# Last linear-attention layer: denominators by groups of four tiles, reciprocals spread by DMA

## The chip, the cores and the metric

The kernel runs on one core of a Trainium2 chip. The metric is the time of one execution in device microseconds (us). Five engines run side by side, each with its own instruction order: TensorE (PE in the profile, its weight loads PEld), VectorE (DVE), ScalarE (ACT), GpSimd (POOL) and SyncE (SP), which here issues the DMAs.

## The reference

The input x has 2048 rows of 512 channels. Four layers follow one another, each with its own layer norm and residual: A, B, A, B. A is softmax attention with 32 heads of width 16 and one shared key and value head. B is linear attention, and its second use, the last layer, is what the change is about.

```python
def _B_ref(x, wqkv, wo):
    ...
    phi = lambda t: jnp.where(t > 0, t + 1, jnp.exp(t)) + 1e-6
    pq, pk = phi(q), phi(k)
    kv = jnp.einsum("bhsd,bhse->bhde", pk, v)
    z = jnp.einsum("bhsd->bhd", pk)
    num = jnp.einsum("bhqd,bhde->bhqe", pq, kv)
    den = jnp.einsum("bhqd,bhd->bhq", pq, z)[..., None] + 1e-6
    o = num / den
    return (lambda x, *d: x.transpose(*d))(o, 0, 2, 1, 3).reshape(B, S, D) @ wo
...
x = A_x
x = x + _A_ref(_layernorm(x, axis=-1), A_wq, A_wk, A_wv, A_wo)
x = x + _B_ref(_layernorm(x, axis=-1), B_wqkv, B_wo)
x = x + _A_ref(_layernorm(x, axis=-1), A_wq, A_wk, A_wv, A_wo)
x = x + _B_ref(_layernorm(x, axis=-1), B_wqkv, B_wo)
```

kv and z sum over all 2048 rows, so no row of a layer B can leave before the last row of the layer A ahead of it has come through.

## The kernel before

The rows are 16 tiles of 128. x stays in SBUF in bf16 over all layers. The program numbers the layers 0 to 3; layers 0 and 2 are A, layers 1 and 3 are B.

**A planner writes the order.** The kernel's Python code doesn't write instructions in the order in which they run. It describes each operation with its engines and their durations, the data that it reads and writes, and a priority, and a small event simulation in the class Planner chooses each engine's order: on a free engine the ready operation with the lowest priority number goes first. Then every engine's list is emitted with semaphore waits where one engine needs another's result. On the chip the order of each engine is fixed, and an instruction that waits holds up all behind it on its engine. The planner's durations are constants of the code; a DMA that spreads reciprocals counts as DBI = 0.7 us on SP and DBL = 1.6 us more until its data are there. TABLE is a list of times on the planner's own clock, at each of which some of its constants take new values: BLS (how much work may wait for VectorE before it takes another block of exponentials), AHEAD, CHT, STICK, HTOL and the like.

**Layers 0 and 2** (run_a) are products of queries and keys on TensorE (line 1205), exponentials, and products with the values (line 1259). The exponentials of 128 x 512 blocks are shared: most go through ScalarE (line 1402), others through an integer approximation on VectorE (line 1506), for which GpSimd makes three shifted copies (line 1548).

**Layers 1 and 3** (run_b) run beside the softmax layer ahead of them as far as their tiles are there: tile_ makes the norm, k and v of a tile, q_ its phi(q) in QT, kvt adds kv and z over groups of tiles (line 1811 z, line 1814 kv). When the last tile has come through, the end stage of a layer B begins, in which nothing of a layer A runs beside layer 3:

- kvt's last group masks kv to its heads' blocks (kvT, line 1847). mix multiplies it with the output weights, into four 128 x 512 matrices M, which are copied from PSUM to SBUF (line 1870). In layer 3 all four copies are on VectorE (MCOP), in layer 1 two of them are on ScalarE (MCO1).
- The denominators of layer 3 are made by den3, for tiles in pairs (DG). z is copied (zs, line 1841) and built into the block matrix Zbd (lines 1844 and 1845), whose 128 columns repeat each head's sum 16 times. So the product of Zbd with QT (line 1895) gives every denominator already spread to the 16 channels of its head. ScalarE takes the logarithm (line 1898) and the exponential of its negative (line 1902), 512 columns per tile, and VectorE multiplies QT by it (line 1906).
- The denominators of layer 1 are made by denc, for four tiles together (DENC). z is masked to ZC (line 1833) and ZD (line 1837), in which each head stands once, and one column-tiled product (line 1929) puts the 8 x 4 heads of four tiles into one PSUM bank. One logarithm (line 1933) and one exponential (line 1934) of that bank give the compact reciprocals rec of the four tiles. norm1 then spreads them to 128 partitions. For tiles 0 to 3 and 12 to 15 (PEX) TensorE does it with a matrix E4 (lines 1972 and 1975), and VectorE multiplies from PSUM (line 1980). For tiles 4 to 11 a DMA on SP's queue writes them to a buffer in SBUF (line 1959), and VectorE multiplies from there (line 1962). The buffers are a pool of three (rb_pool), rec has a pool of two (rec_pool).
- main3 multiplies each tile with the four matrices M (line 878), VectorE adds the result to x (line 2011), and SP stores the tile (line 2036).

The two lines that spread the reciprocals of a tile by DMA and use them:

```python
d = op({SP: (DBI, lambda e: e.dma_start(rb, rec[32 * j:32 * j + 8, :].unsqueeze(1).to_broadcast([8, DH, D])))}, ...
o = op({DV: (0.34, lambda e: e.tensor_tensor(out=q, in0=q, in1=rb, op=ALU.mult))}, ...
```

Of the kernel before, what the change touches and what calls it, by code (L numbers as in the profile page):

```python
# [420 lines left out]
class Seg:  # L421
# [128 lines left out]
MCOP = (DV,)*4  # L550
# [6 lines left out]
PEX = (12, 13, 14, 15)  # L557
# [31 lines left out]
BASE = dict(AHEAD=AHEAD, BLS=BLS, BLT=BLT, BLX=BLX, CHT=CHT, DPP=DPP, DXB=DXB, EVP=EVP, FBS=FBS, HMAX=HMAX, HTOL=HTOL, LOW=LOW, OWNP=OWNP, SPX=SPX, STICK=STICK)  # L589


def bass_interleave_layers__grouped_kv_mqa__linear_attn_block__prompt_kernel(
# [41 lines left out]
    zs = sb("zs", [P, 4], FP32)  # L634
# [1043 lines left out]
    rb_pool = Pool_((6, 7, 8))  # L1678
    rec_pool = Pool_((4, 5))
    rd_pool = Pool_(range(6))  # L1680

    def run_b(L):
# [76 lines left out]
        def q_(t):  # L1759
# [10 lines left out]
            if L == 3 and t == T - 1 and QCL:  # L1770
                claim(PAIRS, "pair")
# [9 lines left out]
        def kvt(gi, ts):  # L1781
# [47 lines left out]
            if end:  # L1829
                mk = mask8[:, :, 0:DH]  # L1830
                v4 = lambda x: x.rearrange("p g (h c) -> p g h c", c=DH)
                if L == 1:
                    o = op({DV: (0.13, lambda e, b=bs[1]: e.tensor_tensor(
                        out=ZC[:].rearrange("p (g c) -> p g c", c=40)[:, :, 0:8], in0=bank(b, 4).unsqueeze(2).to_broadcast([P, 4, 8]),
                        in1=mask8[:, :, 0:1].rearrange("p h o -> p (h o)").unsqueeze(1).to_broadcast([P, 4, 8]), op=ALU.mult))},
                           reads=["mask8"], writes=[B_(bs[1]), "ZC"], prio=pr - 0.05)
                    op({DV: (0.1, lambda e: e.tensor_copy(ZD[:].rearrange("p (g c) -> p g c", c=32)[:, :, 0:8], ZC[:].rearrange("p (g c) -> p g c", c=40)[:, :, 0:8]))},
                       reads=["ZC"], writes=["ZD"], prio=1.6)
                    pl.process(denc(0, DENC[0], bs[1]))
                else:  # L1840
                    o = op({DV: (0.08, lambda e, b=bs[1]: e.tensor_copy(zs[:], bank(b, 4)))}, writes=[B_(bs[1]), "zs"], prio=pr - 0.05)
                    pl.give_after(banks, bs[1], [o])
                    for g in range(4):
                        op({AC: (0.19, lambda e, g=g: e.activation(v4(Zbd)[:, g], mk, ACTF.Copy, scale=zs[:, g:g + 1]))} if g in ZAC else
                           {DV: (0.11, lambda e, g=g: e.tensor_scalar(out=v4(Zbd)[:, g], in0=mk, scalar1=zs[:, g:g + 1], scalar2=None, op0=ALU.mult))},
                           reads=["mask8", "zs"], writes=[("Zbd", g)], prio=0.5 if g in ZAC else pr - 0.05, over=under(ZI))
# [9 lines left out]
        ZK = [("Zbd", g) for g in range(4)]  # L1856
        at = {3: lambda i: W[:, i, :], 1: vm_}[L]
        MK = {3: lambda i: ("W", i), 1: lambda i: ("vm", i)}[L]
        ZI, KI = {3: (44, 45), 1: (4, 5)}[L]
        Zbd = at(ZI).rearrange("p (g c) -> p g c", c=P)  # L1860
# [13 lines left out]

        def take_pairs():
            yield ("flag", TPF)
            claim(PAIRS, "pair")

        def den3(ts):
            pr = 1.5 + 0.02 * ts[0] - 0.01  # L1880
            yield ("flag", ("kv", L, len(KVG) - 1))
            for t in ts:
                yield ("flag", ("bq", L, t))
            yield from until(*[QK_(t) for t in ts], *ZK)
            i = yield ("acq", rd_pool, pr)
            n = len(ts)
            rd = wv_(4 * (5 + i), 4).bitcast(FP32)[:, 0:512 * n]
            b = yield ("acq", pairs if n == 2 else banks, pr)
            src = ps[:, b * 512:(b + n) * 512]
            bk = [B_(b + k) for k in range(n)]  # L1890
            for k, t in enumerate(ts):
                def fn(e, k=k, t=t):
                    ins = None
                    for g in range(4):
                        ins = e.matmul(ps[:, (b + k) * 512 + g * P:(b + k) * 512 + (g + 1) * P], lhsT=Zbd[:, g, :], rhs=QT[:, t, g * P:(g + 1) * P], start=True, stop=True)
                    return ins
                op({PE: (0.23, fn)}, reads=[QK_(t)] + ZK, writes=[bk[k]], prio=pr, lat=0.2).cols = 512
            o = op({AC: (0.203 + 0.427 * n, lambda e: e.activation(rd, src, ACTF.Ln, bias=epsc[:]))}, reads=["epsc"], writes=bk + [("rd", i)], prio=pr,
                   after=[("W", 20 + 4 * i + h) for h in range(4)])
            pl.give_after(pairs if n == 2 else banks, b, [o])  # L1900
            rb = wv_(PT0 + 3 * i, n)
            op({AC: (0.148 + 0.427 * n, lambda e: e.activation(rb, rd, ACTF.Exp, scale=-1.0))}, reads=[("rd", i)], writes=[("rb", i)], prio=pr - (EXF if ts[0] < EXN else EXB), after=[("W", PT0 + 3 * i + h) for h in range(n)])
            os_ = []
            for k, t in enumerate(ts):
                qn = W[:, 4 + t, :]
                os_.append(op({(PO if t in PQ else DV): (PQD if t in PQ else 0.34, lambda e, t=t, k=k, qn=qn: e.tensor_tensor(out=qn, in0=rb[:, 512 * k:512 * (k + 1)], in1=QT[:, t, :], op=ALU.mult))},
                              reads=[("rb", i), QK_(t)], writes=[("qn", t)], prio=pr, after=[("W", 4 + t)]))
                pl.flag(("qn", L, t))
            pl.give_after(rd_pool, i, os_)

        def denc(gi, ts, b=None):
# [28 lines left out]
            if gi:  # L1940
                pl.give_after(banks, b, [o])
                yield ("flag", ("rd1", gi))
# [6 lines left out]
        def norm1(t, i, j, rec, b=None):  # L1949
            pr = 1.5 + 0.02 * t - 0.005 if t else DCP  # L1950
            yield from until(("rec", i))
            if DW[t] is not None:
# [3 lines left out]
            if t >= 4 and t not in PEX:  # L1956
                k = yield ("acq", rb_pool, pr)
                rb = vm_(k) if k < 8 else rbx[:]
                d = op({SP: (DBI, lambda e: e.dma_start(rb, rec[32 * j:32 * j + 8, :].unsqueeze(1).to_broadcast([8, DH, D])))},
                       reads=[("rec", i)], writes=[("rb", k)], prio=pr, lat=DBL, dma=True, over=[("va", k)] if k < 8 else [])  # L1960
# [3 lines left out]
                pl.give_after(rb_pool, k, [o])  # L1964
# [19 lines left out]
            if used[t // 4] == 4:  # L1984
                yield ("ops", [m])
                pl.flag(("rd1", t // 4))

        def main3(t):
# [8 lines left out]
            qn = QT[:, t, :] if L == 1 else W[:, 4 + t, :]  # L1997
# [84 lines left out]
```

## Time and profile before

| what | us |
|---|---|
| median of 3 runs | 1339.75 (1339.72 to 1339.89) |
| the profiled execution | 1339.58 |
| its span, first to last instruction | 1338.1 |
| TensorE, ScalarE, VectorE, GpSimd busy in the span | 1291.6, 1308.2, 1233.7, 1097.9 |

The profile is of one execution. A group's row names the line, the engine, the operation, output and inputs with their shapes and the count, then its busy time and the mean ns of one instruction, then the engine's idle time just ahead of it and what ended that. A row of the timeline gives start and length in us, and several like instructions in a row are one row with their count (x4); in brackets stands a wait ahead of it. A row of a stretch gives its length, each engine's busy time with the number of instructions, the granted TensorE clock, the mean busy share of the 16 DMA engines and their GB/s. SPq is SP's DMA queue; the length there is that of the issue, not of the transfer.

### The profile page before, as it was taken

To read this page: it belongs to the slowest core of one execution; us is meant where nothing else is said; L and a number is where in the kernel's file an instruction comes from. 1 tells how busy PE (TensorE), PEld (TensorE's weight loads), DVE (VectorE), ACT (ScalarE), POOL (GpSimd) and SP (SyncE) were. 2 spreads that over 40 slices of the span, in tenths; PEclk is the share of its full clock that TensorE was granted. 3 is DMA by queue.
4 is the path that set the end of the run, shared out by engine and by line. 5 is a ranking of instruction groups with operands and counts; after the bars stand their busy time and mean duration, and the time that the engine had idled before them with its cause. 6 is when DMAs were issued, how large, how long until landed. Compare 5 with 4: busy or idle time off the path is not lost.

```text
span 1338.1 us, 39100 instructions
## 1 busy us (share of the span) xinstructions
PE 1291.6 (97%) x15353; PEld 430.6 (32%) x15411; DVE 1233.7 (92%) x2227; ACT 1308.2 (98%) x1524; POOL 1097.9 (82%) x1107
## 2 busy tenths in 40 slices
PE   9999999999999999999999999999999999999998
PEld 5222323222232223223732223333233323232235
DVE  8999999999999999997889999999999999999987
ACT  8999999999999999999799999999999999999996
POOL 3799897999989998997017999779899898988980
PEclk9999999999999999999999999999999999999999
DMA  4300000000000000000121000000000000000001
GB/s 112 96 6 13 6 13 6 6 13 2 14 5 14 6 6 6 2 2 2 24 38 21 1 10 10 18 6 6 13 6 9 6 14 6 10 2 1 2 2 64
DMA packets 47076, 20.11 MB, mean 15 GB/s; under 512 B 39728, under 2 KB 46384, under 8 KB 46896
## 3 DMA queue, kind: packets, MB, share of 16 engines
q1 hardware_dynamic: 45840, 17.57, 6.0%
q8 instruction: 125, 2.05, 0.6%
q14 instruction: 55, 0.45, 0.1%
q10 hardware_dynamic: 1056, 0.03, 0.0%
HBM read 5.28 MB, written 2.10 MB: 6 GB/s over the span
## 4 chain that ended last, share of the span: by engine, by line
PE 52%; ACT 30%; issue 8%; DVE 7%; POOL 2%; DMA 1%; SPq 0%; ACTq 0%; POOLq 0%
ACT W L1402 28%; PE ps L1259 22%; PE ps L1205 17%; PE ps L878 4%; DVE W L1506 3%; PE ps L1084 3%; POOL W L1548 2%; PE ps L921 2%; PE ps L1306 1%; ACT phE L1688 1%; DMA va<-va 1%; DVE sacc L1566 1%; PE ps L1814 0%; DMA rbx<-va 0%; DVE st L981 0%
## 5 line engine op out<-in xcount | busy, mean ns | idle before, releaser
L1548 POOL INT64_ADD W<-W x1065 | 1089.2, 1038 | 202.5 <-PE ps L1306 64.8
L1402 ACT ACTIVATE W<-ps 128x1024 bf16<-128x1024 f32 (+1 forms) x1317 | 1245.2, 1131 | 2.4 <-PE ps L1205 2.3
L1506 DVE TENSOR_SCALAR W<-ps 128x512 int16<-128x512 f32 x1420 | 921.6, 682 | 64.9 <-PE ps L1205 50.7
L1259 PE MATMUL ps<-W,VV 128*32 128x512 bf16 x8356 | 635.9, 384 | 4.4 <-DVE sacc L1566 2.8
L1205 PE MATMUL ps<-W,KM 32*128 32x512 bf16 x4096 | 517.3, 385 | 23.2 <-ACT W L1402 13.7
L1205 PEld LDWEIGHTS ps<-W,KM 32*128 32x128 bf16 x4096 | 130.3, 91 | 513.0 <-ACT W L1402 428.4
L1259 PEld LDWEIGHTS ps<-W,VV 128*32 128x32 bf16 x8356 | 151.7, 94 | 257.2 <-issue 170.0
L878 PE MATMUL ps<-wqkv,W 128*128 128x512 bf16 (+1 forms) x226 | 66.0, 368 | 7.7 <-issue 4.3
L1306 PE MATMUL ps<-W,V 128*32 128x512 bf16 (+5 forms) x184 | 52.0, 346 | 0.3 <-DVE W L1506 0.2
L1688 ACT ACTIVATE phE<-ps 128x512 bf16<-128x512 f32 (+1 forms) x66 | 43.8, 665 | 4.5 <-PE ps L1084 3.0
L981 DVE BATCH_NORM_STATS2 st<-x_sb 128x6 f32<-128x512 bf16 x60 | 40.5, 679 | 1.2 <-DMA x_sb<-in_A_x_dram 1.2
L1566 DVE STREAM_TRANSPOSE sacc<-ps 128x512 f32<-128x512 f32 x52 | 36.8, 707 | 3.0 <-PE ps L1259 3.0
L921 PE MATMUL ps<-wo,OT 128*32 128x512 bf16 (+1 forms) x544 | 39.4, 372 | 0.0
L1084 PE MATMUL ps<-W,wqkv 128*128 128x128 bf16 x512 | 38.9, 220 | 0.4 <-DVE W L1695 0.3
L1084 PE MATMUL ps<-W,wq 128*128 128x128 bf16 x464 | 35.1, 221 | 0.4 <-DVE W L1506 0.2
L1084 PEld LDWEIGHTS ps<-W,wqkv 128*128 128x128 bf16 x512 | 29.6, 98 | 11.0 <-issue 8.1
L786 DVE TENSOR_SCALAR phE<-phE 128x513 bf16<-128x513 bf16 x49 | 20.7, 423 | 12.8 <-ACT phE L1688 11.7
L1084 PEld LDWEIGHTS ps<-W,wq 128*128 128x128 bf16 x464 | 26.1, 98 | 12.5 <-issue 8.4
L878 PEld LDWEIGHTS ps<-wqkv,W 128*128 128x128 bf16 x272 | 18.1, 97 | 32.1 <-issue 20.1
L786 DVE TENSOR_SCALAR xn<-x_sb,mv,rs 128x513 bf16<-128x513 bf16 x52 | 26.8, 526 | 0.5 <-ACT rs L972 0.5
L1605 DVE TENSOR_TENSOR Osb<-sacc,ps 128x256 bf16<-128x256 f32 x64 | 26.0, 406 | 0.3
L2011 DVE TENSOR_TENSOR x_sb<-x_sb,ps 128x512 bf16<-128x512 bf16 x30 | 20.4, 682 | 2.5 <-PE ps L878 2.1
(140 smaller groups left out, 483.0 us busy)
## 6 DMA issues: line engine op xcount, KB each, us to landing
out_dram<-x_sb SPq DMA_DIRECT2D x16, 128.0 KB, 1.7
x_sb<-in_A_x_dram SPq DMA_DIRECT2D x6, 256.0 KB, 5.8
wqkv<-in_B_wqkv_dram SPq DMA_DIRECT2D x1, 1536.0 KB, 7.4
va<-va SPq DMA_DIRECT2D x6, 128.0 KB
W<-xn SPq DMA_TRANSPOSE x46, 2.5
x_sb<-in_A_x_dram SPq DMA_DIRECT2D x4, 128.0 KB, 2.2
wq<-in_A_wq_dram SPq DMA_DIRECT2D x1, 512.0 KB, 4.4
wo<-in_A_wo_dram SPq DMA_DIRECT2D x4, 128.0 KB, 3.5
```

The costliest lines, as they stand in the source:

```text
L786: return e.add_instruction(mybir.InstTensorScalarPtr(name=nc.get_next_instruction_name(), engine=mybir.EngineType.DVE, op0=op0, op1=op1, i ...
L878: return e.matmul(dst, lhsT=l, rhs=r, start=(k == 0), stop=(k == len(pairs) - 1))
L921: ins = e.matmul(ps[32 * q:32 * q + 32, b * 512 + cs.start:b * 512 + cs.stop], lhsT=l[:, q, :], rhs=r, start=start, stop=stop)
L1084: ins = e.matmul(dst[:, g * P:(g + 1) * P], lhsT=lhs(g, k), rhs=rhs(k), start=(k == 0), stop=(k == FT - 1))
L1205: return e.matmul(bank(b), lhsT=KM[r, sg.par, kt * P:(kt + 1) * P], rhs=QT[r, sg.t, :], start=True, stop=True)
L1259: ins = e.matmul(ps[32 * j:32 * j + 32, ACC * 512:(ACC + 1) * 512], lhsT=VV[:, kt, 0 if w is None else 1 + w, :], rhs=ap, start=(k == 0), ...
L1306: o = op({PE: (n / 2400.0, lambda e: e.matmul(ps[32 * j:32 * j + 32, b * 512:b * 512 + n], lhsT=V0[:], rhs=QT[:, sg.t, 0:n], start=st, sto ...
L1402: ex = op({AC: (EXO + 0.4267 * n, lambda e, n=n, s_=s_, p_=p_: e.activation(ws_(p_), ps[:, s_ * 512:(s_ + n) * 512], ACTF.Exp, scale=EXPSC ...
L1506: o = op({DV: (0.602, lambda e: e.tensor_scalar(out=dst.bitcast(I16), in0=bank(b), scalar1=VB, scalar2=VLO, op0=ALU.add, op1=ALU.max))}, w ...
L1548: o = op({PO: (512 * m * PSR + PSO, lambda e, g_=g_, f_=f_: e.int64_add(ws_(g_).bitcast(I64), ws_(f_).bitcast(I64), step))}, reads=wk_(f_) ...
L1566: o = op({DV: (TRD, lambda e, src=src: e.transpose(src, bank(ACC)))}, writes=[B_(ACC)] + key, prio=0.0, lat=0.15)
L1688: op({AC: (0.07 + n / 1200.0, lambda e: e.activation(phE[:, i, 0:n], bank(b, n), ACTF.Exp))}, reads=[B_(b)], writes=[("phE", i)], prio=pr ...
```

## The change

Layer 3 takes layer 1's way to the denominators: denc and norm1 serve both, and den3, take_pairs, zs and Zbd go, and with them the pairs of PSUM banks that were set aside for den3. ZC and ZD are made in layer 3 too. Tiles 0 to 3 are spread by TensorE, all of tiles 4 to 15 by DMA (PEX is empty for layer 3), with eleven buffers in place of three. VectorE multiplies in place in QT, where den3 wrote to other blocks. The copies of M take turns between VectorE and ScalarE. In TABLE the entries from 1140 on are replaced by two, at 1110 and 1140, and AHEAD, BLT, CHT and OWNP are no longer varied.

```diff
-MCOP = (DV,)*4
+MCOP = (DV, AC, DV, AC)
...
-PEX = (12, 13, 14, 15)
+PEX = {1: (12, 13, 14, 15), 3: ()}
...
-    (1140, dict(BLS=1.6, BLT=2.5, BLX=2.4, DPP=1.0, DXB=0.0, EVP=0.95, FBS=22, HMAX=0.1, HTOL=0.0, LOW=20, STICK=1.0)),
-    (1170, dict(AHEAD=32, BLS=1.6, BLT=2.5, BLX=2.4, DPP=1.0, DXB=-1, EVP=0.95, FBS=22, HMAX=0.1, HTOL=0.0, LOW=20, OWNP=1.0, STICK=1.0)),
-    (1290, dict(AHEAD=32, BLS=1.6, BLT=2.5, BLX=2.4, CHT=11, DPP=1.0, DXB=-1, EVP=0.95, FBS=22, HMAX=0.1, HTOL=0.0, LOW=20, OWNP=1.0, SPX=1.5, STICK=0.5)),
+    (1110, dict(BLS=1.6, BLX=2.4, DPP=1.0, DXB=0.3, EVP=0.95, FBS=22, HMAX=0.1, HTOL=0.02, LOW=20, STICK=1.0)),
+    (1140, dict(BLS=1.9, BLX=2.4, DPP=1.0, DXB=-1, EVP=0.95, FBS=22, HMAX=0.1, HTOL=0.0, LOW=20, STICK=1.0)),
...
-    rb_pool = Pool_((6, 7, 8))
+    rb_pools = {1: Pool_((6, 7, 8)), 3: Pool_((6, 7, 8) + tuple(range(20, 28)))}
     rec_pool = Pool_((4, 5))
-    rd_pool = Pool_(range(6))
...
-            if L == 3 and t == T - 1 and QCL:
-                claim(PAIRS, "pair")
...
-                if L == 1:
-                    o = op({DV: (0.13, lambda e, b=bs[1]: e.tensor_tensor(
...
-                    pl.process(denc(0, DENC[0], bs[1]))
-                else:
-                    o = op({DV: (0.08, lambda e, b=bs[1]: e.tensor_copy(zs[:], bank(b, 4)))}, writes=[B_(bs[1]), "zs"], prio=pr - 0.05)
...
+                o = op({DV: (0.13, lambda e, b=bs[1]: e.tensor_tensor(
...
+                pl.process(denc(0, DENC[0], bs[1]))
...
-        def take_pairs():
...
-        def den3(ts):
...
-            if t >= 4 and t not in PEX:
-                k = yield ("acq", rb_pool, pr)
-                rb = vm_(k) if k < 8 else rbx[:]
+            if t >= 4 and t not in PEX[L]:
+                k = yield ("acq", rb_pools[L], pr)
+                rb = vm_(k) if k < 8 else rbx[:] if k == 8 else W[:, k, :]
...
-            qn = QT[:, t, :] if L == 1 else W[:, 4 + t, :]
-            keys = [("qn", t)] + [("M", g) for g in range(4)] + [QK_(t)] * (L == 1)
+            qn = QT[:, t, :]
+            keys = [("qn", t)] + [("M", g) for g in range(4)] + [QK_(t)]
...
-        if L == 3:
-            pl.process(take_pairs())
-            for ts in DG:
-                pl.process(den3(ts))
-        else:
-            for gi, ts in enumerate(DENC):
-                if gi:
-                    pl.process(denc(gi, ts))
+        for gi, ts in enumerate(DENC):
+            if gi:
+                pl.process(denc(gi, ts))
```

More of the change, by code (lines that the diff above doesn't have):

```diff
@@ L1873, in mix @@
             pl.flag(("M", L, g))
-        def take_pairs():
-            yield ("flag", TPF)
-            claim(PAIRS, "pair")
-        def den3(ts):
[L1880 to L1909, printed above, removed]
         def denc(gi, ts, b=None):
@@ L1951, in norm1 @@
             yield from until(("rec", i))
-            if DW[t] is not None:
+            if L == 1 and DW[t] is not None:
                 yield ("flag", ("xnT", 2, DW[t]))
@@ L1955, in norm1 @@
             q = QT[:, t, :]
[L1956 to L1958 removed]
+            if t >= 4 and t not in PEX[L]:
+                k = yield ("acq", rb_pools[L], pr)
+                rb = vm_(k) if k < 8 else rbx[:] if k == 8 else W[:, k, :]
                 d = op({SP: (DBI, lambda e: e.dma_start(rb, rec[32 * j:32 * j + 8, :].unsqueeze(1).to_broadcast([8, DH, D])))},
[L1960 removed]
+                       reads=[("rec", i)], writes=[("rb", k)], prio=pr, lat=DBL, dma=True, over=[("va", k)] if k < 8 else [], after=[("W", k)] if k > 8 else [])
                 yield ("ops", [d])
```

28 lines of the change are left out of this document (10 added, 18 removed).

## The prediction

> **What bounds the kernel now.** I read the page first, then the stretches, then the chain and the timeline behind the last exponential, and last the place where the kernel already does in layer 1 what the change brings to layer 3.
>
> ```profile
> PE 1291.6 (97%) x15353; PEld 430.6 (32%) x15411; DVE 1233.7 (92%) x2227; ACT 1308.2 (98%) x1524; POOL 1097.9 (82%) x1107
> ...
> L1402 ACT ACTIVATE W<-ps 128x1024 bf16<-128x1024 f32 (+1 forms) x1317 | 1245.2, 1131 | 2.4 <-PE ps L1205 2.3
> L1506 DVE TENSOR_SCALAR W<-ps 128x512 int16<-128x512 f32 x1420 | 921.6, 682 | 64.9 <-PE ps L1205 50.7
> ```
>
> Busy times of the whole span, then two groups with count, busy time and mean ns: ScalarE and TensorE are full over the span, and most of it is the softmax exponentials, shared by ScalarE (L1402) and VectorE (L1506). The last exponential ends at about 1303. The change touches what lies behind it, and the planner's constants in the last 190 us ahead of it. In stretches (columns PE, PEld, DVE, ACT, POOL, clock, DMA share, GB/s):
>
> ```profile
> 1110.00:1303.20 193.20, 187.97 (x2283) 59.11 (x2284) 177.10 (x311) 193.20 (x221) 172.92 (x169) 1.00 0.02 4
> ```
> ```profile
> 1315.00:1320.00 5.00, 4.72 (x49) 3.23 (x51) 4.50 (x10) 4.97 (x6) 0.00 (x0) 1.00 0.00 2
> 1320.00:1325.00 5.00, 4.95 (x46) 3.14 (x46) 4.62 (x12) 5.00 (x6) 0.00 (x0) 1.00 0.36 119
> 1325.00:1330.00 5.00, 4.95 (x29) 2.42 (x29) 4.53 (x10) 4.57 (x6) 0.00 (x0) 1.00 0.35 118
> ```
>
> In the end stage three engines are nearly full side by side, and DMA does nothing but the stores. Its work, by groups from 1313 to the end:
>
> ```profile
> L2011 DVE TENSOR_TENSOR x_sb<-x_sb,ps 128x512 bf16<-128x512 bf16 x16 | 11.0, 684 | 1.6 <-PE ps L878 1.3
> L1898 ACT ACTIVATE W<-ps,epsc 128x1024 f32<-128x1024 f32 x7 | 7.6, 1116 | 0.8 <-PE ps L1895 0.8
> L1902 ACT ACTIVATE W<-W 128x1024 bf16<-128x1024 f32 x7 | 7.2, 1066 | 0.0
> L1906 DVE TENSOR_TENSOR W<-W 128x512 bf16<-128x512 bf16 x16 | 6.1, 418 | 0.0
> ```
>
> Each tile costs VectorE a multiplication (0.42) and a residual addition (0.68), about 1.0 us a tile with their overlap. That is the pace at which tiles leave.
>
> ```profile
> 1313.48 0.16 DVE L1841 COPY zs<-ps 128x4 f32<-128x4 f32 x1 [0.42 <-PE ps L1811]
> 1313.68 0.58 DVE L1845 TENSOR_SCALAR W<-mask,zs 128x128 bf16<-128x128 bf16 x3
> 1314.06 0.60 ACT L1688 ACTIVATE phE<-ps 128x512 bf16<-128x512 f32 x1
> ...
> 1315.35 2.48 DVE L1870 CAST W<-ps 128x512 bf16<-128x512 f32 x4 [0.28 <-PE ps L1895]
> ...
> 1318.25 1.89 PE L878 MATMUL ps<-W 128*128 128x512 bf16 x8
> ...
> 1331.70 0.42 DVE L1906 TENSOR_TENSOR W<-W 128x512 bf16<-128x512 bf16 x1
> ...
> 1333.31 0.68 DVE L2011 TENSOR_TENSOR x_sb<-x_sb,ps 128x512 bf16<-128x512 bf16 x1
> ...
> 1335.05 0.69 DVE L2011 TENSOR_TENSOR x_sb<-x_sb,ps 128x512 bf16<-128x512 bf16 x1 [0.18 <-PE ps L878]
> ```
>
> The sum of z is complete at 1313.48, the first output product starts at 1318.25, the last addition at 1335.05, and the span ends at 1338.1: 3.05 after that start, most of it the last store.
>
> **The change part by part.** It does in layer 3 what layer 1 does; layer 1 gives the durations:
>
> ```profile
> L1933 ACT ACTIVATE ps<-ps,epsc x4: 338/660/662, 646.3 to 678.0; 128x512 f32<-128x512 f32 x3, 128x128 f32<-128x128 f32 x1
> ```
> ```profile
> L1934 ACT ACTIVATE va<-ps x3: 597/597/603, 649.4 to 678.8; 128x512 bf16<-128x512 f32 x3
> L1934 ACT ACTIVATE rec<-ps x1: 278/278/278, 646.7 to 646.7; 128x128 bf16<-128x128 f32 x1
> ```
> ```profile
> L1870 ACT CAST va<-ps x2: 586/586/586, 647.0 to 648.0; 128x512 bf16<-128x512 f32 x2
> ```
> ```profile
> L1980 DVE TENSOR_TENSOR W<-W,ps x8: 651/676/689, 648.0 to 716.9; 128x512 bf16<-128x512 bf16 x8
> ```
> ```profile
> L1962 DVE TENSOR_TENSOR W<-W,va x6: 408/422/426, 658.4 to 688.0; 128x512 bf16<-128x512 bf16 x6
> ```
> ```profile
> 645.33 0.20 DVE L1833 TENSOR_TENSOR ZC<-ps,mask 128x32 bf16<-128x32 f32 x1
> ```
>
> ScalarE loses the wide logarithms and exponentials (7.6 + 7.2 us for the pairs, two single tiles beside them) and gets 0.34 + 0.28 for the first group, 3 x (0.66 + 0.60) for the others and two copies of the mixed matrix, 1.17: some 5.6 us in place of about 17. VectorE loses zs (0.16), three builds of Zbd (0.58) and two of the four copies (1.24), gets ZC and ZD (0.20 each, ZD taken as ZC), and its multiplications of tiles 0 to 3 read PSUM, 4 x (0.68 - 0.42) = 1.04 more. The sum is -0.54 us. TensorE loses most of its denominator products. If nothing else changed, the end stage would stay at VectorE's pace and gain 0.5 to 2 us (its idle time there, 5.00 - 4.50 and the like, could close too).
>
> **The transfers** are the other half. Each of tiles 4 to 15 now waits for a DMA of its own that spreads 8 rows of reciprocals over 128 partitions. Layer 1 has 8 of these (its tiles 12 to 15 go by TensorE instead). Its issues and the waits behind them:
>
> ```profile
> 650.04 1.48 SPq L1959 DMA_DIRECT2D va<-va  x2
> 651.57 1.88 SPq L1959 DMA_DIRECT2D rbx<-va  x1
> ```
> ```profile
> 658.88 0.61 SPq L1959 DMA_DIRECT2D va<-va  x1
> ```
> ```profile
> 663.61 0.61 SPq L1959 DMA_DIRECT2D va<-va  x1
> 664.31 0.61 SPq L1959 DMA_DIRECT2D rbx<-va  x1
> ```
> ```profile
> 663.33 0.43 DVE L1962 TENSOR_TENSOR W<-W,va 128x512 bf16<-128x512 bf16 x1 [0.49 <-DMA va<-va]
> ...
> 670.43 0.42 DVE L1962 TENSOR_TENSOR W<-W,rbx 128x512 bf16<-128x512 bf16 x1 [1.91 <-DMA rbx<-va]
> ```
>
> VectorE sits idle until 663.33 for an issue at 658.88, 4.45 us earlier, and until 670.43 for one at 664.31. What the DMA engines did meanwhile (share of the 16 engines, GB/s), each stretch cut at the slices of 0.1 us in which the traffic starts and stops (the fourth row is the empty slice ahead of the second):
>
> ```profile
> 651.40:659.00 7.60, 1.00 0.43 54
> 660.10:662.90 2.80, 1.00 0.42 47
> 664.80:670.00 5.20, 1.00 0.40 50
> ```
> ```profile
> 660.00:660.10 0.10, 1.00 0.00 0
> ```
> ```profile
> 1335.60:1336.30 0.70, 1.00 0.54 187
> ```
>
> One transfer alone takes 2.8 us of traffic, two take 5.2, three take 7.6: with one, two or three outstanding the share stays at 0.40 to 0.43 and the rate at 47 to 54 GB/s. They run one behind another, 2.6 us each (15.6 us over 6). A store of the same 128 KB, last row, fills all engines for 0.54 x 0.70 = 0.38 us. The first data come 1.2 to 1.4 us behind the issue, and the reader goes 0.45 us behind the end of the traffic. The Trainium skill's page "DMA: Bandwidth & Descriptors" says (section "Why a DMA increments its semaphore by 16 and not by 1") that a DMA runs on the largest number of engines, 16 at most, that divides the outermost sizes, 8 here; the share of 0.42 agrees, but by that rule alone the store's rate on half the engines would give an estimated 0.76 us each. Its section on the anatomy of a DMA gives, for the GpSimd path, 2.0 us and bytes over 436 GB/s, an estimated 2.3 us of which 0.3 is data; the rows above contradict that for these transfers.
>
> Twelve transfers at 2.6 are 31.2 us, in a stage in which VectorE has 16 tiles at about 1.0 us. So they set the end. **The sum**, on the axis of the profiled execution:
>
> - First issue. ScalarE from 1314.06: phi's exponential 0.60, group 0's 0.34 + 0.28, then group 1's 0.66 + 0.60 and two copies of 0.59, all ready by then or just behind: 3.66, so 1317.7. If group 1 goes before both copies, 1316.5; by layer 1's distance from ZC (645.33) to the first issue (650.04) it would be 1318.2. I take 1317.75.
> - Data from 1319.0 (+1.25). Twelve transfers to 1350.2; between 2.5 and 2.8 each, 1349.0 to 1352.6.
> - Stores on the same engines and queue: by the planner's order about eight stand ahead of the last spread, 8 x 0.38 = 3.0, to 1353.2. Below: nothing, as the spreads leave half of the share free. Above: 12, 4.5.
> - Reader's wait 0.45, 1353.65. From a tile's multiplication to its addition 1.61 (1331.70 to 1333.31): 1355.26. From there 3.05 to the span's end: 1358.3.
> - Outside the span 1339.58 - 1338.1 = 1.48; the profiled execution lies 0.17 under the median of 1339.75. Together 1359.95, said as 1360.
>
> The waits are in order on VectorE: behind the multiplication of tile t stand the additions of a tile or two before it and their stores. They come late with it, but end within the 1.61 of the last tile. On ScalarE the third group's exponential waits until the first group's row buffer has been read, at about 1330; nothing of weight is behind it, and the second group's transfers last until about 1341. SP issues 12 x 0.61 and 16 stores, under the time of the traffic. The additions saved on ScalarE and TensorE are worth nothing then: both wait for spreads. TensorE will stand still for most of each 2.6 us:
>
> ```profile
> 1.27 3.92 PE L1190 MATMUL ps<-zz 128*128 128x128 bf16 x35 [1.27 <-POOL wts L823]
> ```
> ```profile
> 1317.29 1.12 PE L1190 MATMUL ps<-zz 128*128 128x128 bf16 x17
> ```
>
> At the start of the program the same small product takes 0.112 us, here 0.066; if it falls back to that pace, the last tile's four products cost up to 0.8 more. I take zero and keep it above.
>
> **The table.** The new constants apply from 1110 of the planner's own clock. ScalarE is full there (193.20 of 193.20), so only a shift of exponentials to VectorE gains. VectorE has 16.1 us idle, at most 24 blocks of 0.68, and a block is some 0.5 us of ScalarE (half of 1131 ns): 12 us at the very most, and the same the other way. The rows can't tell the sign: a looser backlog limit (1.9 for 1.6) favours VectorE, a smaller lead (20 for 32) does not. I take 0, within 4 either way.
>
> **The rivals.**
> - *Hidden transfers* (0.07): transfers from different rows and to the many new buffers run side by side, or at the store's rate, so that twelve take under 10 us. Then VectorE's pace holds: 1339.75 less about 1.2, 1338.5, with the table's 4 either way. It decides if a spread costs under about 1.3 us of traffic. Against it: three outstanding in layer 1, from three different row groups to two tensors, went no faster than one. The skill's 2.3 us formula gives this time.
> - *Two side by side* (0.06): 1.3 each, 15.6 in all; the sum then gives about 1344.
> - *Stores in the way* (0.03): if SP's order puts a store that waits for tile t-1 ahead of the spread of tile t, the round of issue, data, wait, product, addition and store adds up to 1.25 + 2.6 + 0.45 + 1.61 + 0.69, about 6.6 us instead of 2.6, 4.0 more for each such place: four of them give 1376. Against: the plan counts 0.7 us for a spread and lets eight tiles run ahead.
> - *The change doesn't do it*: were some of tiles 4 to 15 spread by TensorE, each would take 2.6 off; the condition in norm1 with an empty tuple for layer 3 excludes that.
>
> **How the numbers follow.** The serial transfers get 0.84, at 1360. Low end: early issue -1.2, 2.5 each -1.2, no cost of stores -3, table -4: 1350.6. High end: issue +0.5, 2.8 each +2.4, stores +1.5, slow products +0.8, table +4: 1369. Not all fall together, so 1350 to 1367; the rivals' 0.16 lies outside. A measurement of this kernel can tell 0.2%, 2.7 us. Of the hidden case a little under half is faster by more than that and the rest mostly the same: 0.04 faster, 0.05 same, 0.91 slower.
>
> **What would show it.** In the changed profile: 12 spread issues behind 1317; DMA share near 0.45 without a gap for 30 us, with the rate near 50 GB/s and peaks from stores; VectorE waiting for DMA at L1962's counterpart, over 15 us in all; ScalarE and TensorE well under half busy in the last 20 us; first product about 1 us earlier than 1318.25. Wrong would be a share near 0.9 with several outstanding, or VectorE still full. The table is right at zero if the last exponential ends within 4 us of where it did.

## The result, and the profile after

| kernel | median us | lowest to highest | runs | ratio to before (95% interval) |
|---|---|---|---|---|
| before | 1339.82 | 1339.72 to 1341.47 | 4 | 1 |
| after | 1357.77 | 1356.14 to 1357.89 | 4 | 1.013 (1.0115 to 1.0145) |

The changed kernel is 18 us slower. The profiled execution's span is 1356.2, against 1338.1 before, so 18.1 us are to be found in the trace. First the page of the changed kernel, the same rows as shown of before:

```profile
PE 1309.3 (97%) x15422; PEld 427.8 (32%) x15422; DVE 1233.5 (91%) x2223; ACT 1296.6 (96%) x1515; POOL 1097.6 (81%) x1107
...
L1400 ACT ACTIVATE W<-ps 128x1024 bf16<-128x1024 f32 (+1 forms) x1317 | 1245.2, 1130 | 2.4 <-PE ps L1203 2.1
L1504 DVE TENSOR_SCALAR W<-ps 128x512 int16<-128x512 f32 x1420 | 922.4, 683 | 63.6 <-PE ps L1203 49.8
...
L876 PE MATMUL ps<-W 128*128 128x512 bf16 x64 | 23.7, 519 | 11.9 <-DVE W L1911 11.9
```

The page hides the change almost entirely. ScalarE still has 1317 exponentials and VectorE 1420, so the new table moved none of them between the two. ScalarE's saved work in the last layer is there (1296.6 for 1308.2, 11.6 us), and yet the time rose. TensorE's busy time went up by 17.7 us. Hardly any of that is added work: the trace of before lacks 58 matmul records (15353 beside 15411 weight loads, where the changed kernel has 15422 of both), and the 64 output products of the last layer (last row) take 519 ns each where before they took 380. One has to go to the stretches behind the last exponential (columns PE, PEld, DVE, ACT, POOL, clock, DMA share, GB/s):

```profile
1315.00:1320.00 5.00, 4.91 (x42) 2.85 (x41) 5.00 (x9) 2.43 (x5) 0.00 (x0) 1.00 0.21 29
1320.00:1325.00 5.00, 3.36 (x36) 1.44 (x33) 1.82 (x4) 0.66 (x1) 0.00 (x0) 1.00 0.45 74
1325.00:1330.00 5.00, 2.52 (x8) 0.75 (x8) 1.45 (x3) 0.60 (x1) 0.00 (x0) 0.79 0.49 106
1330.00:1335.00 5.00, 3.31 (x8) 0.87 (x8) 2.04 (x4) 0.00 (x0) 0.00 (x0) 0.50 0.46 65
```

Before, VectorE was busy 4.5 of each 5 us in these stretches, ScalarE full, and DMA carried stores alone. Now VectorE works 1.45 to 2.04 of 5 us, ScalarE next to nothing, and the DMA engines stay at a share of 0.45 to 0.49 in each of these stretches from 1320 on. The waits of the changed kernel from 1312 to the end (engine, tile and line that waited, what released it; us in all, times, the longest):

```profile
DVE W L1911 <- DMA W<-va: 14.3, 8, 2.3
...
DVE W L1911 <- DMA va<-va: 3.7, 3, 1.9
...
DVE W L1911 <- DMA rbx<-va: 1.9, 1, 1.9
```

Twelve waits (8 + 3 + 1), one for each tile that a DMA spreads, 19.9 us together. Line 1911 is the multiplication by the spread reciprocals (line 1962 before). The timeline of the changed kernel (start, length, what ran, in brackets the wait ahead of it) gives the terms of the sum:

```profile
1312.64 0.21 DVE L1827 TENSOR_TENSOR ZC<-ps,mask 128x32 bf16<-128x32 f32 x1 [0.42 <-PE ps L1806]
...
1316.31 1.29 SPq L1908 DMA_DIRECT2D va<-va  x2
...
1320.82 0.42 DVE L1911 TENSOR_TENSOR W<-W,va 128x512 bf16<-128x512 bf16 x1 [0.45 <-DMA va<-va]
...
1323.64 1.04 PE L876 MATMUL ps<-W 128*128 128x512 bf16 x4 [0.96 <-DVE W L1911]
1325.99 1.04 PE L876 MATMUL ps<-W 128*128 128x512 bf16 x4 [1.31 <-DVE W L1911]
1328.52 1.89 PE L876 MATMUL ps<-W 128*128 128x512 bf16 x4 [1.49 <-DVE W L1911]
...
1350.93 0.42 DVE L1911 TENSOR_TENSOR W<-W,va 128x512 bf16<-128x512 bf16 x1 [1.94 <-DMA va<-va]
...
1353.34 0.69 DVE L1960 TENSOR_TENSOR x_sb<-x_sb,ps 128x512 bf16<-128x512 bf16 x1 [0.79 <-PE ps L876]
```

The twelve multiplications start between 1320.82 and 1350.93, that is 30.11 / 11 = 2.74 us a tile. The last addition starts 18.29 us later than before (1353.34 for 1335.05). The three rows of TensorE show a second thing: four output products take 1.04 us, and from 1328.52 on 1.89, and the clock column above falls from 1.00 to 0.50 there. TensorE looks busier because it works at half its clock, between waits.

The start of the multiplication that makes ZC (before: the copy zs) lies anywhere from 1312.64 to 1315.81 in the kernels of this document, though hardly anything ahead of it differs. So the end stage is compared by the time from there to the end of the span: 24.6 us before (1338.1 - 1313.48), 43.6 after (1356.2 - 1312.64). This is called the length of the end stage below. It is from one execution each. The ratios are against runs of before on the same chip.

### The profile page after: what moved, and what is told of

Same layout as the page of the kernel before. It is cut to its first block, busy times and chain, and to the rows that moved or that the text cites. A ratio compares the mean times of both kernels' runs of the same rounds, so it can differ in the third digit from the quotient of the medians.

```text
span 1356.2 us, 39184 instructions
## 1 busy us (share of the span) xinstructions
PE 1309.3 (97%) x15422; PEld 427.8 (32%) x15422; DVE 1233.5 (91%) x2223; ACT 1296.6 (96%) x1515; POOL 1097.6 (81%) x1107
## 4 chain that ended last, share of the span: by engine, by line
PE 58%; ACT 22%; DVE 6%; issue 6%; POOL 4%; DMA 2%; SPq 1%; ACTq 0%; POOLq 0%
PE ps L1257 26%; ACT W L1400 21%; PE ps L1203 20%; PE ps L876 5%; POOL W L1546 4%; DVE W L1504 3%; PE ps L1082 3%; PE ps L919 2%; PE ps L1304 2%; DMA va<-va 1%; SPq L1908 1%; ACT phE L1685 1%; DVE sacc L1564 1%; PE ps L1188 0%; PE ps L1809 0%
## 5 line engine op out<-in xcount | busy, mean ns | idle before, releaser
L876 PE MATMUL ps<-wqkv,W 128*128 128x512 bf16 (+1 forms) x272 | 77.3, 371 | 1.0 <-DVE sacc L1692 1.0
L1304 PE MATMUL ps<-W,V 128*32 128x512 bf16 (+6 forms) x178 | 50.8, 346 | 0.3 <-DVE W L1504 0.2
L1564 DVE STREAM_TRANSPOSE sacc<-ps 128x512 f32<-128x512 f32 x52 | 36.9, 709 | 5.7 <-PE ps L1257 5.6
L876 PE MATMUL ps<-W 128*128 128x512 bf16 x64 | 23.7, 519 | 11.9 <-DVE W L1911 11.9
```

The source lines that it names most:

```text
L876: return e.matmul(dst, lhsT=l, rhs=r, start=(k == 0), stop=(k == len(pairs) - 1))
L1304: o = op({PE: (n / 2400.0, lambda e: e.matmul(ps[32 * j:32 * j + 32, b * 512:b * 512 + n], lhsT=V0[:], rhs=QT[:, sg.t, 0:n], start=st, sto ...
L1564: o = op({DV: (TRD, lambda e, src=src: e.transpose(src, bank(ACC)))}, writes=[B_(ACC)] + key, prio=0.0, lat=0.15)
```

## The experiments

| kernel | what differs | median us | ratio to before (95% interval) | end stage us |
|---|---|---|---|---|
| e1 | tiles 4 to 15 spread by TensorE | 1341.18 | 1.0008 (0.9998 to 1.0018) | 25.7 |
| e2 | before, with the new table | 1340.55 | 1.0001 (0.9992 to 1.0010) | 24.6 |
| e3 | 16 rows in a spread | 1342.53 | 1.0017 (1.0008 to 1.0026) | 26.4 |
| e4 | two spreads of 4 rows | 1381.76 (one run) | | 65.2 |
| e5 | half of the spreads on ScalarE's queue | 1351.60 (one run) | | 36.9 |
| e6 | TensorE kept busy | 1361.38 | 1.0158 (1.0144 to 1.0172) | 46.5 |
| e11 | TensorE kept busy, same order | 1357.71 | 1.0131 (1.0115 to 1.0146) | 42.9 |
| e7 | e3, tiles 4 to 7 by TensorE | 1339.97 | 1.0000 (0.9992 to 1.0009) | 25.0 |
| e8 | e7 with the old table | 1346.22 | 1.0043 (1.0031 to 1.0056) | 29.7 |
| e9 | e7 with a third buffer of reciprocals | 1344.59 | 1.0034 (1.0021 to 1.0046) | 29.7 |
| e10 | e9, every other tile by TensorE | 1342.47 | 1.0019 (1.0010 to 1.0028) | 27.8 |
| e12 | e9 with phi(q) of tile 15 earlier | 1339.23 | 0.9995 (0.9986 to 1.0005) | 23.5 |

**e1: no spread by DMA.** Only the list of tiles that TensorE spreads is changed; all else of the change stays.

```diff
-PEX = {1: (12, 13, 14, 15), 3: ()}
+PEX = {1: (12, 13, 14, 15), 3: tuple(range(4, 16))}
```

> The changed kernel with one tuple changed: all tiles of layer 3 are spread by TensorE, none by DMA. Theory (the serial transfers are the whole loss): the end stage is at VectorE's pace again, now 0.62 + 0.62 us a tile with both reading PSUM, 19.8 us from the end of the copies of M at 1316.1, so the last addition starts near 1335.3 and the time is about 1340 (1338 to 1342). Rival (another part of the change, such as the table, the copies on ScalarE or the shared logarithms, carries part of the 18 us): over 1345.

Its time was 1341.18, and the stretches of e1 show why:

```profile
1320.00:1325.00 5.00, 4.95 (x24) 2.16 (x24) 5.00 (x10) 0.00 (x0) 0.00 (x0) 1.00 0.38 130
1325.00:1330.00 5.00, 4.94 (x42) 2.31 (x42) 5.00 (x9) 1.26 (x2) 0.00 (x0) 1.00 0.31 106
```

VectorE is full again (5.00 of 5.00), TensorE too at full clock, and the DMA does the stores alone. Without the twelve DMAs nearly all of the loss is gone. What is left is 1.1 us in the end stage (25.7 for 24.6). In e1 all multiplications read PSUM, which costs VectorE 12 x 0.26 = 3.1 us for tiles 4 to 15 (0.68 for 0.42), so the rest of the change would save about 2.0; that is an estimate, not a measurement.

**e2: the table alone**, put into the kernel before, in place of its entries from 1140 on.

```diff
-    (1140, dict(BLS=1.6, BLT=2.5, ...
-    (1170, dict(AHEAD=32, ...
-    (1290, dict(AHEAD=32, ...
+    (1110, dict(BLS=1.6, BLX=2.4, DPP=1.0, DXB=0.3, EVP=0.95, FBS=22, HMAX=0.1, HTOL=0.02, LOW=20, STICK=1.0)),
+    (1140, dict(BLS=1.9, BLX=2.4, DPP=1.0, DXB=-1, EVP=0.95, FBS=22, HMAX=0.1, HTOL=0.0, LOW=20, STICK=1.0)),
```

> The kernel before with the new TABLE entries alone; den3 and its order stay. In the profile of the changed kernel the sum of z was complete 0.84 us earlier than before (1312.64 against 1313.48), but four variants with the same stretch ahead of it had it anywhere from 1313.02 to 1314.81. Theory (the table does next to nothing): within 1 us of the kernel before. Rival 1 (the 0.84 is the table's gain): about 1339.0. Rival 2 (the table costs): over 1341.

The ratio is 1.0001 (0.9992 to 1.0010), and the end stage is 24.6 as before. With the denominators of before, the table is worth nothing that these runs can tell; e8 shows below that with those of the change it does place one instruction of the end stage.

**e3 and e4: how many rows a spread has.** The reciprocals of a tile lie in 8 rows, and each row is written 16 times. In e3 each head stands twice in ZD, so that the reciprocals lie in 16 rows, each written 8 times. In e4 the 8 rows go in two DMAs of 4. The bytes written are the same.

```diff
-rec[32 * j:32 * j + 8, :].unsqueeze(1).to_broadcast([8, DH, D])
+rec[32 * j:32 * j + nr, :].unsqueeze(1).to_broadcast([nr, P // nr, D])    # e3: nr = 16 in layer 3
...
-e.dma_start(rb, rec[32 * j:32 * j + 8, :]...
+e.dma_start(rb[64 * h:64 * h + 64, :], rec[32 * j + 4 * h:32 * j + 4 * h + 4, :].unsqueeze(1).to_broadcast([4, DH, D])) for h in 0, 1    # e4
```

> The changed kernel, but in layer 3 ZD holds each head twice, so that a tile's reciprocals lie in 16 rows and each row is repeated 8 times instead of 8 rows 16 times. Same bytes, same destination. Theory (the number of rows sets how many DMA engines work, each at its own pace): share near 0.9, about 100 GB/s, 1.3 us a transfer, with stores 1.55 a tile, so the time is about 1343 (1341 to 1346). Rival (the pace is set by the queue or by the bytes that are read or written, not by the number of engines): 2.6 us a transfer and 1356 to 1358.

> The changed kernel, but in layer 3 each spread is two DMAs of 4 rows in place of one of 8. Same bytes. Theory (rows set the engines, and both halves land on the same ones): share near 0.23, 25 GB/s, 5.2 us a tile, the time about 1388. If the two halves go to different engines, or if the pace is one of bytes: 1356 to 1359.

The traffic alone, before a store joins it, first in the changed kernel (8 rows), then in e3 (16 rows), then a long stretch of e4 (4 rows, stores among them). The last three columns are clock, share and GB/s, the first the stretch and its length (the second and third row are of SP alone, without other engines):

```profile
1319.00:1321.00 2.00, 1.95 (x16) 1.06 (x14) 1.55 (x4) 0.00 (x0) 0.00 (x0) 1.00 0.41 50
```
```profile
1319.30:1320.60 1.30, 1.00 0.78 105
```
```profile
1330.00:1370.00 40.00, 0.59 0.28 58
```

Twice the rows give about twice the share and twice the rate: 0.41 and 50 GB/s with 8, 0.78 and 105 GB/s with 16 (0.9 and 100 were expected). With 4 the share falls to 0.28, stores included. The pace in e3 is read at its first and last multiplication by a DMA's output:

```profile
1322.01 0.42 DVE L1915 TENSOR_TENSOR W<-W,va 128x512 bf16<-128x512 bf16 x1
...
1336.42 0.43 DVE L1915 TENSOR_TENSOR W<-W,va 128x512 bf16<-128x512 bf16 x1 [0.90 <-DMA va<-va]
```

That is 14.41 / 11 = 1.31 us a tile, about half of the changed kernel's 2.74 and almost down to VectorE's own 1.0. VectorE came to the first of them without a wait, so 1.31 is not the pace of the transfers alone. In e4 the pairs of spreads leave SP 4.8 us apart:

```profile
1339.51 2.46 SPq L1912 DMA_DIRECT2D W<-va  x2
...
1344.31 2.66 SPq L1912 DMA_DIRECT2D W<-va  x2
...
1349.10 2.76 SPq L1912 DMA_DIRECT2D W<-va  x2
```

5.2 us and a time of about 1388 were expected, 4.8 and 1381.76 came. So the number of rows in the outermost dimension of a spread sets its duration: 4.8 us a tile with 4, 2.74 with 8 and 1.31 with 16, stores included in each, the bytes being the same. The Trainium skill's page "DMA: Bandwidth & Descriptors" has this rule (section "Why a DMA increments its semaphore by 16 and not by 1": a DMA uses the largest number of engines up to 16 that divides both outermost sizes), and here the shares follow it: 0.41 with 8 rows, 0.78 with 16, and 0.28 with 4, in which the stores have a part.

The number of engines is not the whole price. With 16 rows a spread still takes 128 KB at 105 GB/s, 1.25 us, where a store of the same bytes was put at 0.38. A busy engine moves 50 / (0.41 x 16) = 7.6 GB/s in a spread of 8 rows and 105 / (0.78 x 16) = 8.4 in one of 16, and 187 / (0.54 x 16) = 21.6 in a store. In these runs the number of engines and the number of rows that are read at a time change together, so it stays open which of the two holds the rate, and why an engine is this slow in a spread.

**e5: a second queue.** The spreads of odd tiles are issued by ScalarE, the others by SP. The DMA semaphores are handed out in the order of the planned times, since there are now two queues.

```diff
-d = op({SP: (DBI, ...
+d = op({AC if L == 3 and t % 2 else SP: (DBI, ...
...
-dmas = [o for e in (AC, SP) for o in self.order[e] if o.isdma]
+dmas = sorted([o for e in (AC, SP) for o in self.order[e] if o.isdma], key=lambda o: o.due)
```

> The changed kernel, but in layer 3 the spreads of odd tiles are issued on ScalarE's DMA queue, those of even tiles on SP's. Theory (both queues feed the same 8 engines): no more than 2 us from 1357.8, share still 0.4 to 0.5 between stores. Rival (one queue works through its transfers one by one, and two would run side by side): about 1344 and a share near 0.9.

Neither theory met it. The first and last multiplication of e5:

```profile
1321.22 0.43 DVE L1911 TENSOR_TENSOR W<-W,va 128x512 bf16<-128x512 bf16 x1 [0.45 <-DMA va<-va]
...
1344.95 0.42 DVE L1911 TENSOR_TENSOR W<-W,va 128x512 bf16<-128x512 bf16 x1
```

23.73 / 11 = 2.16 us a tile, a fifth less than 2.74, and 6 us in the time of the kernel; a second queue was expected to change nothing or to double the rate. The DMA view of e5 from 1316 to 1346 (packets, MB, share of the engines by queue; q10 is ScalarE's, six spreads and nothing else), and of the changed kernel from 1316 to 1351:

```profile
q1 hardware_dynamic: 2545, 2.37, 33.9%
q10 hardware_dynamic: 816, 0.79, 15.3%
```
```profile
q1 hardware_dynamic: 3148, 2.96, 45.9%
```

The six spreads on ScalarE's queue took 0.153 x 16 x 30 = 73 us of engine time, 12 each. A spread alone on SP's queue takes 0.42 x 16 x 2.6 = 17 (from layer 1). All queues together, e5 took 0.492 x 16 x 30 = 236 us of engine time for 3361 packets, the changed kernel 0.459 x 16 x 35 = 257 for 3148. So the engines are hardly more busy at a time (49.2% for 45.9%), but a packet takes less of that time when another queue works beside it. The Trainium skill says otherwise (same page, section "Issuing engines are not separate DMA queues": several issuing engines save only the time to issue); the one run of e5 disagrees, since its packets take less engine time too, and since the time to issue is not what held the changed kernel back: e3 issues the same twelve spreads on SP alone at 1.31 us a tile. Why the packets take less, and whether the stores' place behind the spreads on SP or the rows that two spreads read at once have a part in it, wasn't separated and stays open. The second queue also has a price: ScalarE stands still while it issues, here for 5.47 us:

```profile
1325.81 0.66 ACT L1882 ACTIVATE ps<-ps,epsc 128x512 f32<-128x512 f32 x1 [5.47 <-issue]
```

**e6 and e11: the halved clock.** Ahead of the products of each of tiles 4 to 15 TensorE gets 24 small products whose result nobody reads, so that it isn't idle. In e6 the planner counts 0.05 us for them and 0.2 more until their result is there, in e11 0.0001 and nothing more, which leaves the order of the last group's denominators as it was.

```diff
+if L == 3 and t >= 4:
+    def idle(e):
+        ins = None
+        for _ in range(24):
+            ins = e.matmul(bank(b, P), lhsT=zz[:], rhs=zz[:], start=True, stop=True)
+        return ins
+    op({PE: (0.05, idle)}, reads=["zz"], writes=[B_(b)], prio=pr, lat=0.2)    # e11: 0.0001, lat=0.0
```

> The changed kernel, with 24 small products on zeros ahead of each tile's four output products from tile 4 on, so that TensorE isn't idle while it waits for a spread. Theory (of the 1.0 us a tile that TensorE waits, nothing is on the path but the last tile's products at the halved clock): the granted clock stays at 1.0, the last tile goes from multiplication to addition in 1.6 us instead of 2.4, and the time falls by 0.8, to 1357.0; the transfers keep their pace. Rival (the slow clock is on the path of every tile): over 3 us faster.

> e6 again, but with the added products counted as nothing by the planner, so that the order of the last group's denominators stays that of the changed kernel (in e6 it slid behind tile 11 and the transfers stood still meanwhile). Theory (the halved clock is on the path of the last tile alone): granted clock 1.0 to the end, last multiplication to last addition 1.6 us instead of 2.4, transfers at the same pace, time 1357.0. Rival (the slow clock is on every tile's path): 1354 or less.

e6 was 3.6 us slower than the changed kernel's 1357.77, so its time tells nothing of what the clock costs. Its planner moved the last group's denominators (line 1878) behind tile 11, and VectorE then waited for the spreads that came after them:

```profile
1340.99 0.41 PE L1878 MATMUL ps<-W,ZD 128*32 128x128 bf16 x16
...
1343.55 3.02 SPq L1908 DMA_DIRECT2D W<-va  x3
...
1348.12 0.43 DVE L1911 TENSOR_TENSOR W<-W 128x512 bf16<-128x512 bf16 x1 [6.33 <-DMA W<-va]
```

These small counts in the plan of e6 cost more than the thing to be measured. e11 kept the order. Its timeline at the end:

```profile
1351.38 0.43 DVE L1911 TENSOR_TENSOR W<-W,va 128x512 bf16<-128x512 bf16 x1 [1.59 <-DMA va<-va]
1351.73 1.91 DVE L1967 TENSOR_TENSOR x_sb<-x_sb,ps 128x512 bf16<-128x512 bf16 x3
```

Three additions in 1.91 us, 0.68 each with an overlap: the last starts at about 1352.95, 1.6 us behind the multiplication, where the changed kernel has 2.41. The clock of e11 stays at 1.00, in the first row below, where the changed kernel has 0.50:

```profile
1328.00:1340.00 12.00, 10.74 (x138) 8.26 (x135) 3.49 (x7) 0.60 (x1) 0.00 (x0) 1.00 0.49 85
```
```profile
1328.00:1340.00 12.00, 7.72 (x17) 1.87 (x18) 4.14 (x9) 0.60 (x1) 0.00 (x0) 0.50 0.48 86
```

So the halved clock costs 0.8 us, at the last tile alone: the distance from the first to the last multiplication stays 30 us, as all the other tiles' products lie beside transfers. The end stage is 0.6 shorter (42.94 for 43.56). The time of 1357.0 that was expected didn't come (1357.71 and 1357.77); runs of one kernel scatter by more than the 0.8, so the times can't show it.

**e7 to e10 and e12: looking for a version that wins.** They combine 16 rows with TensorE for some tiles, and the planner counts 2.4 us for a transfer in layer 3 in place of 1.6. In e7 and e8 tiles 4 to 7 are spread by TensorE from the doubled rows with the matrix for the plain ones, so their denominators are not the reference's; the amount of work is that of the full kernel. e9, e10 and e12 keep a plain copy of the rows for these tiles in further columns of ZD, and buffer 6 goes from the pool of spread reciprocals to that of compact ones.

```diff
-PEX = {1: (12, 13, 14, 15), 3: ()}
+PEX = {1: (12, 13, 14, 15), 3: (4, 5, 6, 7)}    # e10: (4, 6, 8, 10, 12, 14)
...
-rec_pool = Pool_((4, 5))
+rec_pools = {1: Pool_((4, 5)), 3: Pool_((4, 5, 6))}    # e9, e10, e12
...
-QLP = 1.9
+QLP = 1.28    # e12 alone: the priority of phi(q) of tile 15
```

> The changed kernel with 16 rows for a spread as in e3, tiles 4 to 7 spread by TensorE, tiles 8 to 15 by DMA, and the planner told 2.4 us in place of 1.6 for these DMAs. Theory: eight transfers at 1.5 with stores are done by about 1331, ahead of VectorE's need, and VectorE's pace holds with 0.36 us a tile less on eight of them than e1 by 0.26 each: 2 us under e1, about 1339, at or just under the kernel before. Rival (the transfers still set the end): over 1341.

> e7 with the old TABLE and its base. Theory (the table does next to nothing): within 1 us of e7. Rival: 0.8 us and more over e7 if the new table gains, as much under it if it costs.

> e7 with a third buffer for compact reciprocals, so that the last group's needn't wait for the first group's to be read, and with the plain rows kept beside the doubled ones for the tiles that TensorE spreads. In e7 the last four transfers were issued from 1327 on, 8 us behind the first, and VectorE waited 1.1 us for the last. Theory: eight transfers follow one another from the start, VectorE's pace holds to the end, and from the sum of z to the end of the span it takes 23.7 us where e7 took 25.0 and the kernel before 24.6: about 1 us under the kernel before. Rival (the shared stage is bound by something else by now): no change from e7.

> e9, but TensorE spreads tiles 4, 6, 8, 10, 12 and 14, and DMA tiles 5, 7, 9, 11, 13 and 15. Theory: six transfers are never late, VectorE pays 2 x 0.26 more than e9: 24.2 us from the sum of z to the end, between e9 and the kernel before. Rival: if transfers early in the stage are late, VectorE waits at tile 5 and 7, and it takes over 25.

> e9 with one priority changed (QLP 1.28 instead of 1.9), so that phi(q) of tile 15 goes early on VectorE and the last group's denominators with it. In e9 and e10 that one multiplication stood at 1328.8 and 1330.7, and the four tiles of the last group waited for it: VectorE was idle for 4.98 us in e9. Theory: the eight transfers follow one another, 23.7 us from the sum of z to the end of the span against 24.6 in the kernel before, and a time about 1 us under it, too little to tell from the scatter of the stretch ahead. Rival (something else of the new order costs as much): 25 us or more.

e7 is level with before. Its three followers missed what was expected: e8 was to stay within 1 us of e7 and is 6 us slower, e9 was to be 1 us under before and is 4.6 slower than e7, and e10's end stage was to take 24.2 us and took 27.8. In e8 and e9 the end stage is 4.8 and 4.7 us longer than e7's; the rest of e8's 6 us lies outside the end stage, where runs of one kernel scatter. These 4.8 and 4.7 us have one place. In e8 and in e9 the multiplication that ends phi(q) of tile 15 (here line 1693 and line 1692) runs late, and the last group of denominators, which holds tile 15, waits for it with all of its four spreads. e8, then e9:

```profile
1330.64 0.68 DVE L1693 SCALAR_TENSOR_TENSOR W<-ps,phE 128x512 bf16<-128x512 f32 x1
...
1333.30 3.19 SPq L1913 DMA_DIRECT2D W<-va  x4
...
1336.66 0.43 DVE L1916 TENSOR_TENSOR W<-W 128x512 bf16<-128x512 bf16 x1 [4.74 <-DMA W<-va]
```
```profile
1328.83 0.68 DVE L1692 SCALAR_TENSOR_TENSOR W<-ps,phE 128x512 bf16<-128x512 f32 x1
...
1331.51 3.75 SPq L1915 DMA_DIRECT2D W<-va  x4
...
1335.68 0.76 DVE L1918 TENSOR_TENSOR W<-W 128x512 bf16<-128x512 bf16 x2 [4.98 <-DMA W<-va]
```

In e10 it is the same multiplication, and the two tiles of that group that TensorE spreads wait as well, so it wasn't an early transfer that came late, as the rival had it:

```profile
1330.68 0.68 DVE L1692 SCALAR_TENSOR_TENSOR W<-ps,phE 128x512 bf16<-128x512 f32 x1
...
1335.03 1.28 DVE L1937 TENSOR_TENSOR W<-W,ps 128x512 bf16<-128x512 bf16 x2 [1.60 <-PE ps L1929]
```

The third buffer of e9 was meant to let that group start earlier; it could not, since the group had nothing to read. e12 raises the priority of that one multiplication and changes nothing else of e9:

```profile
1315.33 0.68 DVE L1692 SCALAR_TENSOR_TENSOR W<-ps,phE 128x512 bf16<-128x512 f32 x1
```
```profile
1325.00:1330.00 5.00, 5.00 (x32) 2.52 (x30) 5.00 (x12) 0.00 (x0) 0.00 (x0) 1.00 0.82 169
```

VectorE is full there, no multiplication waits for a transfer, and the end stage is 23.5 us, the shortest of all (23.7 were expected). In time, 1339.23 for 1339.60, the interval includes 1. So the change's idea can be made harmless, with perhaps 1 us of gain in the end stage that these runs can't show in the time.

## Why the prediction was right

The time of 1357.77 is 2.2 us under the predicted 1360 and well inside the range, and the mechanism is the one that was named. Step by step:

- *The transfers run one behind another and set the end.* Shown: the share of 0.45 to 0.49 in stretches of 5 us and the waits of 19.9 us on VectorE (over 15 were foretold) in the changed kernel, and the loss gone in e1. e3 and e4 add what layer 1 couldn't tell: it is the 8 rows that hold a spread to a share of 0.41, where 16 rows have 0.78.
- *2.6 us each and 3.0 for eight stores.* Measured 30.11 for eleven intervals with their stores, where the step has 11 x 2.6 + 3.0 = 31.6: 1.49 too much. Eight stores did stand ahead of the last spread, so with spreads at 2.6 a store would have cost (30.11 - 28.6) / 8 = 0.19, half of the 0.38. That part of a store fits into the share that the spreads leave free would explain it; spreads of 2.46 with stores at 0.38 give the same sum, and the runs don't separate the two.
- *First issue at 1317.75, first data used at 1322.05.* Measured 1316.31 and 1320.82, 1.23 early at the multiplication. z came 0.84 earlier, and ScalarE's chain ahead of the issue took 3.1 us in place of 3.7, as its instructions overlap. The 0.84 is chance: the place of z moves by 3 us between these kernels.
- *1.61 from the last multiplication to its addition.* Measured 2.41. Here the prediction took zero for the slower products and kept 0.8 above; it was the 0.80. This is the term that was decided wrongly, and e11, at full clock, has about 1.6.
- *3.05 to the end of the span.* Measured 2.86, 0.19 less.
- The terms' errors, -1.23 - 1.49 + 0.80 - 0.19 = -2.11, are the whole difference between the predicted span of 1358.3 and 1356.2. The slow products hide part of what was put too high elsewhere, so the nearness of the total owes something to luck; added up without signs the errors are 3.7 us, still inside the range.
- *Body of the change worth 0.5 to 2 us if the transfers were free.* e12's end stage is 1.1 us shorter than before (23.5 for 24.6), with e1 1.1 longer as VectorE reads PSUM. Both fit the estimate, from profiles of one execution each; the change with free transfers for all twelve tiles wasn't run.
- *Table zero, within 4.* e2: 1.0001 (0.9992 to 1.0010), that is from -1.1 to +1.3 us, in the kernel before. The changed kernel with the old table wasn't run. In e8 the old table costs 4.8 us of the end stage, so zero is not a property of the table alone.
- *SP's issues of 0.61 lie under the traffic.* The conclusion held, the number didn't. From 1332.63 on a spread's issue takes 1.8 to 2.5 us, and SP issues without a pause until the last stores:

```profile
1332.63 2.50 SPq L1908 DMA_DIRECT2D W<-va  x1
...
1335.68 2.39 SPq L1908 DMA_DIRECT2D W<-va  x1
```

  In layer 1 seven of eight issues took 0.6 to 0.8 us with the same 2.6 us of traffic, and the third in a row 1.88 (a row of the prediction). In e3 the issues of spreads from 1324.52 on take 0.55 to 1.03. So the pace is not SP's; that an issue waits for room in the queue would explain its length, but that wasn't tested.
- *The rivals.* Hidden transfers (1338.5) were to need under 1.3 us a spread, and two side by side at 1.3 us were to give 1344. e3, at 1.31 us, comes out at 1342.5: near the second, so that 1.3 us is not yet hidden. Stores in the way of spreads did not occur: no two neighbours among the twelve multiplications start more than 3.4 us apart, where such a place was to take 6.6.
- *The signs.* ScalarE and TensorE were to be well under half busy in the last 20 us. ScalarE was; TensorE was not, with 7.72 of the 12 us from 1328 (row above). Its four products a tile took 1.89 us at the halved clock in place of 1.04.

## What to carry to other kernels

Before a DMA is costed, read its outermost dimension: here one that broadcasts 8 rows had a share of 0.41 and 50 GB/s, and the same bytes from 16 rows 0.78 and 105 GB/s. Even then it was far from the 187 GB/s of a store, so take the price from a transfer of the same kind. A planner that gives a DMA a time on its issuing engine and a latency, but no time on the DMA engines, lets any number of them run side by side; where several are outstanding, the sum over them has to be set against the stage that is to hide them. Work done for a group waits for the group's last member, so what makes that member (here phi(q) of tile 15) needs the priority of the whole group.

## What the runs showed of the hardware

- TensorE's granted clock halved without a long pause. In the changed kernel TensorE paused for 0.96 us and for 1.31 and still ran at full clock; after the next pause, of 1.49, the clock was at half and stayed there, with TensorE busy 7.72 of 12 us (rows above). In e3, with pauses of at most 0.96 us, it stayed at 1.00. The length of a pause alone doesn't decide: in e5 the clock still read 1.00 from 1329 to 1331, while TensorE did nothing (rows below; columns as above).

```profile
1329.00:1330.00 1.00, 0.00 (x0) 0.00 (x0) 0.00 (x0) 0.00 (x0) 0.00 (x0) 1.00 0.40 74
1330.00:1331.00 1.00, 0.00 (x0) 0.00 (x0) 0.00 (x0) 0.00 (x0) 0.00 (x0) 1.00 0.37 94
```

  The Trainium skill's page "TensorE: Matmul & The Clock Gate" (section "What's actually happening") puts the fall to half behind an idle window of about 3.4 us; the end stage of the changed kernel has no pause near that length ahead of the fall.
- Two queues were a fifth faster than one (e5, one run), with about the same share of busy time: 49.2% for 45.9%.
